# Attention, a rational layer and routed experts: fixed PSUM banks for routing, an early block two steps sooner, and the order of two branches of code

## The chip, the cores and the metric

The kernel runs on one core of one Trainium2 chip. The metric is the device time of one execution in microseconds (us), the median of three runs. The core has five engines with instruction queues of their own: TensorE (PE: matrix products, with the weight loads as PEld), VectorE (DVE), ScalarE (ACT), GpSimd (POOL) and SyncE (SP, which here issues DMAs). Each executes its own queue in order. A wait at the head of a queue holds up all that is queued behind it.

## The reference

Three parts follow one another. An attention with a position bias (4 batches, 8 heads, 576 positions, 64 wide) gives 2304 tokens of 512. A rational layer takes them through 2048 hidden columns, and a routed layer of 8 experts sends each token to the one expert with the largest logit.

```python
def rational(x):                      # 2304 x 512, hidden 2048
    h = x @ w_in
    P = a[0] + a[1] * h + a[2] * h * h + a[3] * h * h * h
    Q = 1.0 + abs(b[0]) * abs(h) + abs(b[1]) * h * h
    return (P / (Q + 1e-6)) @ w_out

def experts(x):                       # 8 experts, 512 -> 1024 -> 512
    logits = x @ w_gate + modality_bias[modality_id]
    e_idx = argmax(logits); gate = softmax(logits)[e_idx]
    for e in range(8):
        out[e_idx == e] = gate * (maximum(x[e_idx == e] @ w1[e], 0) @ w2[e])
```

With these inputs the experts get 0, 8, 0, 0, 2171, 0, 0 and 125 tokens: one gets nearly all, two get a few, five get none. Which is which the kernel learns at run time.

## The kernel before

**Products in two parts.** Where accuracy matters, an operand is split into a rounded part and its remainder, and a product becomes three (high by high, high by remainder, remainder by high).

**The rational layer** (function `moe`) works on six token tiles of 384 tokens (`NTT`, index t from 0) with 16 chunks of hidden columns each (`NF`, index f). One loop runs over steps G = 16 t + f, 0 to 100, and its body writes out the order of work on every engine by hand. In step G, TensorE computes the first product of chunk G (`mm1(G)`, twelve matmuls, line 671) and the second product of an older chunk (`mm2(G - 5)`, twelve matmuls, line 754). Between them ScalarE and VectorE compute the rational function, pair by pair: `first` (ACT, lines 635 to 637), `den` (DVE, 645), `poly` (DVE, 641 and 642), `inv` (ACT, 649 and 650), `quot` (DVE, 654 to 656), `high` (ACT, 660) and `low` (DVE, 664, the remainder). h is read last by `poly`, one step after `mm1`.

**PSUM.** The pool `pst` has eight banks: two of name "tr", two of "av", and two tiles of two banks of name "sc". h of step G is in "av" where G % 3 = 1 (and for G = 3), else in "tr". "sc" holds the sums of `mm2`. A pool hands out the two buffers of a name in turn, and a new tile waits until its buffer's last user is done.

**Routing of a token tile** runs in steps 4 to 9 of the next tile: `evac` (f = 4) copies the sums; `logit` (5), `choice` (6), the first of three `rows` (7: four transposes, line 793, and an ACT copy, 794), `route` (7: the argmax on DVE with an exp on ACT), `place` (8: the place of each token in its expert's table, small products at lines 832 to 841 and DVE work from 843 to 854), the second and third `rows` (8 and 9), `scatter` (9: three indirect DMAs on POOL, line 858) and `put` (9: three POOL scalings and three stores by SP). Each of these products takes its own "av" tile. In the last tile of the loop POOL and ACT also split the weights of the largest expert (`wa_split`, lines 932 and 933), one sixteenth per step.

**The early block.** Rows of the largest expert that are known after five token tiles, 384 of them, are gathered in step 92 (`ids_gather(early)`, line 1021). `block_x` transposes them (line 1033, bank "av"), copies the rounded part on ACT (1036) and the remainder on DVE (1037), for four chunks of 128 columns. `split_h` computes one of eight hidden chunks of them (twelve matmuls, line 1050, then ACT 1059 and DVE 1060). In the loop's steps 97 to 100 these stand between the last `mm2`; the rest, and the routing of the last token tile, follow the loop. `split_y` (line 1071) is the block's second product; before its last part, `block_x` for the next rows needs a gather that waits for the last tile's scatters and stores.

**The experts.** `level(b)`, nested `If`s, works through the largest expert in blocks of 256. Then `large(1)` (line 1378) takes the other experts, largest first. If the first has over 32 tokens (125 here) and the second hasn't (8 here), `block` computes the first and `few`, a generator, the second beside it: `next(beside)` issues its next part. `few` has four parts (products at lines 1343, 1350, 1357 and 1362). Each ends in an indirect store to `out` (lines 1096 and 1365), and a store to `out` waits for the one before it. `chain`, `ahead` and `small` are further `If`s that are not entered with these counts. The code of an `If` stands first, that of its `Else` behind it.

Of the kernel before, what the change touches and what calls it, by code (L numbers as in the profile page):

```python
# [22 lines left out]
P = 128  # L23
# [651 lines left out]
def moe(ctx, tc, k, ins, x2_d, out):  # L675
# [41 lines left out]

    st, c0 = k.st, k.const

    def mm1(G):  # L720
        t, f = divmod(G, NF)
        r = tiles[t]
        if G not in st:
            c = st[G] = K()
            c.h = pb.tile([P, 512], F32, name="av" if G == 3 or G % 3 == 1 else "tr")
            mm1_chunk(nc, k, r, f, c.h)

    g_of_h = Rational(nc, k)
# [36 lines left out]
    def logit(t):  # L765

        r = tiles[t]
        ps = pb.tile([P, 512], F32, name="av")
        for dc in range(4):
            nc.tensor.matmul(ps[32 * dc:32 * dc + 32, 0:NB], k.gate[:, dc], r.x2[:, dc], start=True, stop=True)  # L770
        r.lt = rt.tile([P, NB], F32, name="lt", bufs=1)
        nc.scalar.copy(r.lt, ps[:, 0:NB])

    def choice(t):

        r = tiles[t]
        ps = pb.tile([P, 512], F32, name="av")
        lps = ps[:, 0:3 * NE].rearrange("p (c e) -> p c e", c=3)
        for c in range(3):
            nc.tensor.matmul(lps[:, c], r.lt[:, c * P:(c + 1) * P], k.sum4[:, 0:NE], start=True, stop=True)  # L780
        r.lg = rt.tile([P, 3, NE], F32, name="lg", bufs=1)
        nc.vector.tensor_tensor(r.lg, lps, k.mbias[:, 3 * t:3 * t + 3], ALU.add)

    def rows(t, c):

        r = tiles[t]
        xr = rt.tile([P, 516], F32, name="xr", bufs=3)
        if c == 0:
            r.xr = []
        r.xr.append(xr)  # L790
        ps = pb.tile([P, 512], F32, name="av")
        for dc in range(4):
            nc.tensor.transpose(ps[:, dc * P:(dc + 1) * P], r.x2[:, dc, c * P:(c + 1) * P], k.idf)
        nc.scalar.copy(xr[:, 0:512], ps)
# [31 lines left out]
    def place(t):  # L826

        r = tiles[t]
        ps = pb.tile([P, 512], F32, name="av")
        for c in range(3):  # L830
            o = ps[:, c * NE:(c + 1) * NE]
            nc.tensor.matmul(o, k.lower, r.ohb[:, c], start=True, stop=False)
            for before in range(c):
                nc.tensor.matmul(o, k.ones, r.ohb[:, before], start=False, stop=False)
            nc.tensor.matmul(o, k.ones, k.cum, start=False, stop=True)
        if t >= NTT - 3:

            o = ps[:, 3 * NE:4 * NE]
            for c in range(3):
                nc.tensor.matmul(o, k.ones, r.ohb[:, c], start=c == 0, stop=False)  # L840
            nc.tensor.matmul(o, k.ones, k.cum, start=False, stop=True)
        sl = rt.tile([P, 3, NE], F32, name="sl", bufs=1)
        nc.vector.tensor_tensor(sl, ps[:, 0:3 * NE].rearrange("p (c e) -> p c e", c=3), k.base, ALU.add)
        nc.vector.tensor_tensor(sl, sl, r.oh, ALU.mult)
        sf = rt.tile([P, 3], F32, name="sf", bufs=1)
        nc.vector.tensor_reduce(sf, sl, mybir.AxisListType.X, ALU.add)
        r.si = rt.tile([P, 3], I32, name="si", bufs=2)
        nc.vector.tensor_copy(r.si, sf)
        if t >= NTT - 3:
            k.count = c0.tile([P, NE], F32, name=f"count{t}")  # L850
            nc.vector.tensor_copy(k.count, o)
        if t < NTT - 1:
            for c in range(3):
                nc.vector.tensor_tensor(k.cum, k.cum, r.ohb[:, c], ALU.add)  # L854

    def scatter(t, c):
        si = tiles[t].si
        nc.gpsimd.indirect_dma_start(k.tab[c], bass.IndirectOffsetOnAxis(ap=si[:, c:c + 1].bitcast(U32), axis=0),  # L858
                                     k.ids[:, 3 * t + c:3 * t + c + 1], None)
# [120 lines left out]
    def early_cols():  # L980
        c = K()
        c.xh, c.xl = ([early_tile()[:, :, 0:3 * P] for _ in range(2)] for _ in range(2))
        return c
# [136 lines left out]
    for G in range(NG + 5):  # L1120
# [6 lines left out]
            split_x(t + 1, f - 12)  # L1127
        if G < NG:
            mm1(G)
        if G == NG + 1:  # L1130
            ecol = early_cols()
            block_x(early, ecol, True, (0, 1))
        if G > NG + 1:
            split_h(early, ecol, G - NG - 2, None)

        g, k2 = G - 1, G // 2 - 1
        if G % 2 == 0:
# [16 lines left out]
        for g in (G - 5, G - 4):  # L1154
            if 0 <= g < NG and G == g + (4 if g < 2 else 5):
                mm2(g)
        if G == NG + 1:
            block_x(early, ecol, True, (2, 3))
        if 1 <= t < NTT:
            if f == 4:  # L1160
                evac(t - 1)
            if f == 5:
                logit(t - 1)
            if f == 6:
                choice(t - 1)
            if f == 7:
                route(t - 1)
            if f == 8:
                place(t - 1)
            if f in (7, 8, 9):  # L1170
                rows(t - 1, f - 7)
            if f == 9:
                for c in range(3):
                    scatter(t - 1, c)
                put(t - 1)
        if G == S1 - 3:
            pick()
# [22 lines left out]

    t = NTT - 1
    evac(t)
    split_h(early, ecol, 3, cp)
    logit(t)
    split_h(early, ecol, 4, cp)
    choice(t)
    route(t)
    split_h(early, ecol, 5, cp)
    place(t)
    for c in range(3):  # L1210
        scatter(t, c)
    for c in range(3):
        rows(t, c)
    split_h(early, ecol, 6, cp)
    put(t)
    split_h(early, ecol, 7, cp)
    order()
    for n in range(2):
# [93 lines left out]
    def block(r, c, ws, beside=()):  # L1312

        beside = iter(beside)
        next(beside, None)
        for f in range(8):
            plain_h(r, c, ws, f, cp)
        next(beside, None)
        for f in range(8):
            plain_y(r, ws, f)  # L1320
            if f in (1, 4):
                next(beside, None)
        block_out(r, cp)

# [53 lines left out]
    def large(p):  # L1378
        if p < NE:
            i = (p - 1) % 2  # L1380
            with tc.If(cnt[p - 1] > 32) as many:
                if p == 1:

                    with tc.If(cnt[1] > 32) as two:
                        block(halves[0], hcols[0], wsets[0])
                        chain(1)
                        large(2)
                    with two.Else():
                        block(halves[0], hcols[0], wsets[0], few(halves[1], hcols[1], wsets[1]))
                        chain(1)  # L1390
                        ahead(3)
                        small(3)
                else:
                    columns(p)
                    ahead(p + 1)
                    block(halves[i], hcols[i], wsets[i])
                    chain(p)
                    large(p + 1)
            with many.Else():
                small(p)  # L1400
# [136 lines left out]
```

## Time and profile before

| | us |
|---|---|
| median of 3 runs (lowest to highest) | 1087.4 (1084.71 to 1088.28) |
| the profiled execution: its own time | 1089.3 |
| its span, first to last instruction | 1087.5 |
| TensorE matmul busy | 1021.7 (94%) |
| TensorE weight load busy | 888.3 (82%) |
| VectorE busy | 753.4 (69%) |
| ScalarE busy | 651.1 (60%) |
| GpSimd busy | 281.7 (26%) |
| mean granted clock of TensorE | 0.986 |

Times within the execution are us from the start of the span. The routed layer's loop ends at about 843, the blocks of the largest expert at about 1045. "issue" as a releaser means that the engine waited for nothing that the profile shows; a q behind an engine's name (PEldq, POOLq) marks instructions of its queue that do no work on data, such as branches and semaphore waits. "A <- B" is a wait of A that B ended.

### The profile page before, as it was taken

What the parts mean: (1) busy time and instruction counts of PE and PEld (TensorE: products, weight loads), DVE (VectorE), ACT (ScalarE), POOL (GpSimd) and SP (SyncE); (2) the same over time, 40 slices, a digit from 0 to 9 for tenths busy, and PEclk for the clock granted to TensorE, in tenths of its full rate; (3) what the DMA queues carried; (4) which work ended last, traced back from release to release, by engine and by line L of the source; (5) the groups of instructions that cost most, each with busy time, mean ns of one, the idle gap of its engine ahead of it and who ended that gap; (6) DMA issues with size and microseconds to landing.
All of it is one profiled execution on the core that took longest, in us unless ns stands there. A gap on an engine that the chain in (4) does not pass through costs nothing. (4 is left out here: it accounts for less than half of the span.)

```text
span 1087.5 us, 19123 instructions
## 1 busy us (share of the span) xinstructions
PE 1021.7 (94%) x6804; PEld 888.3 (82%) x6804; DVE 753.4 (69%) x1544; ACT 651.1 (60%) x1283; POOL 281.7 (26%) x449
## 2 busy tenths in 40 slices
PE   6889999999999999999999999999897989999984
PEld 4657777777777779989999999998797879999962
DVE  7978998888888858888978888889884321112200
ACT  6778778878888756767666666666563221122210
POOL 3434343443433300103012021021361142122100
PEclk9999999999999999999999999999998999999998
DMA  5886876775653344005022031041250366211100
GB/s 160 292 263 169 231 239 187 222 204 146 172 157 112 101 166 184 30 1 31 30 20 40 1 30 30 1 30 58 59 98 1 30 219 203 76 48 51 39 24 16
DMA packets 122078, 113.41 MB, mean 104 GB/s; under 512 B 65055, under 2 KB 94495, under 8 KB 121952
## 3 DMA queue, kind: packets, MB, share of 16 engines
q1 hardware_dynamic: 117828, 101.53, 35.0%
q0 software_dynamic: 3728, 10.25, 3.0%
q8 instruction: 63, 1.03, 0.5%
q14 instruction: 63, 0.52, 0.2%
q10 hardware_dynamic: 396, 0.08, 0.0%
HBM read 78.09 MB, written 33.79 MB: 103 GB/s over the span
## 5 line engine op out<-in xcount | busy, mean ns | idle before, releaser
L754 PE MATMUL sc<-gh,w_b 128*128 128x384 f32 x752 | 209.8, 340 | 2.7 <-ACT x L761 2.7
L754 PEld LDWEIGHTS sc<-gh,w_b 128*128 128x128 f32 x752 | 139.5, 190 | 3.3 <-ACT x L761 3.3
L754 PE MATMUL sc<-gl,w_b 128*128 128x384 f32 x376 | 127.9, 340 | 0.1
L393 PEld LDWEIGHTS tr<-idf,e 128*128 128x128 f32 x576 | 80.6, 207 | 49.2 <-issue 25.0
L351 ACT ACTIVATE e<-e,st 128x576 f32<-128x576 f32 x144 | 112.2, 779 | 13.6 <-DVE st L346 11.8
L346 DVE CUSTOM_DVE_ANT_0 e<-sc,bias_s 128x576 f32<-128x576 f32 x144 | 107.6, 748 | 5.1 <-PE sc L330 3.8
L370 ACT COPY aT<-tr 128x512 f32<-128x512 f32 x144 | 84.4, 586 | 44.5 <-PE tr L393 42.7
L1060 DVE SCALAR_TENSOR_TENSOR hl<-tr,hh 128x256 fp32r<-128x256 f32 x56 | 23.8, 425 | 122.8 <-ACT hh L1059 110.6
L671 PE MATMUL tr<-kn,w_a 128*128 128x384 f32 x372 | 107.7, 344 | 0.4 <-DVE t L642 0.4
L393 PE MATMUL tr<-idf,e 128*128 128x128 f32 x576 | 104.6, 304 | 1.7 <-DVE kk L311 0.9
L330 PE MATMUL sc<-kk,qS 128*128 128x288 f32 x512 | 99.1, 315 | 0.7 <-DVE st L346 0.7
L660 ACT CAST gh<-t 128x768 fp32r<-128x768 f32 x47 | 39.3, 835 | 87.8 <-DVE t L656 85.6
L436 PE MATMUL av<-aT,vn 128*64 128x320 f32 (+1 forms) x512 | 82.8, 424 | 0.0
L1050 PE MATMUL tr<-kn,w_a 128*128 128x256 f32 x448 | 81.5, 280 | 1.2 <-DVE hl L1060 1.2
L330 PEld LDWEIGHTS sc<-kk,qS 128*128 128x128 f32 x512 | 72.9, 191 | 2.2 <-DVE st L346 1.0
L858 POOL DMA_INDIRECT tab<-ids,si x18 | 21.6, 1201 | 197.6 <-DVE cum L854 170.3
L754 PEld LDWEIGHTS sc<-gl,w_b 128*128 128x128 f32 x376 | 71.6, 190 | 0.4 <-DVE gl L664 0.4
L671 PEld LDWEIGHTS tr<-kn,w_a 128*128 128x128 f32 x372 | 68.9, 190 | 3.3 <-issue 2.3
L1050 PEld LDWEIGHTS tr<-kn,w_a 128*128 128x128 f32 x448 | 69.7, 188 | 1.7 <-DVE hl L1060 1.4
L1071 PE MATMUL sc<-w_a,hh 128*128 128x512 f32 x224 | 70.9, 393 | 0.0
L366 POOL TENSOR_SCALAR rb<-st 128x128 f32<-128x128 f32 x80 | 23.8, 298 | 170.8 <-DVE st L364 154.2
L654 DVE SCALAR_TENSOR_TENSOR t<-t,coef,r 128x768 f32<-128x768 f32 x47 | 48.2, 1025 | 24.6 <-ACT r L650 24.6
(303 smaller groups left out, 2539.2 us busy)
## 6 DMA issues: line engine op xcount, KB each, us to landing
bias_d<-bo SPq DMA_DIRECT2D x36, 295.5 KB
kn<-in_k_dram SPq DMA_DIRECT2D x64, 128.0 KB
cst<-in_moe_w_out_dram SPq DMA_DIRECT2D x16, 512.0 KB
wo_d<-cvw SPq DMA_DIRECT2D x16, 512.0 KB
cst<-in_moe_w_in_dram SPq DMA_DIRECT2D x16, 512.0 KB
w_b<-wo_d SPq DMA_DIRECT2D x16, 512.0 KB
w_b<-in_moe_w_dram SPq DMA_DIRECT2D x16, 512.0 KB
x_d<-xr SPq DMA_DIRECT2D x18, 256.5 KB
```

The lines of the kernel that those rows point to most:

```text
L330: nc.tensor.matmul(ps[:, hf, 0:HF], st, mv[:, hf * HF:(hf + 1) * HF], start=n == 0, stop=n == last)
L346: nc.vector.tensor_tensor_reduce(out=ev, in0=ps[:, :, 0:HF], in1=bv, scale=-1.0, scalar=3.0e38, op0=ALU.add, op1=ALU.min, accum_out=st[:, ...
L351: nc.scalar.activation(e, e, AF.Exp, bias=st[:, 0:1], scale=-1.0, accum_out=st[:, 1:2])
L370: nc.scalar.copy(dst, src)
L393: nc.tensor.transpose(ps[:, c * P:(c + 1) * P], both[:, e0 + c % 2:e0 + 2 * P:2], k.idf)
L436: nc.tensor.matmul(r.av[64 * hd:64 * hd + 64, 0:w], st, mv, start=c == 0, stop=c == 4)
L654: nc.vector.scalar_tensor_tensor(q.t, q.t, co[:, 0:1], q.r, ALU.add, ALU.mult)
L660: self.nc.scalar.copy(gh, q.t)
L671: nc.tensor.matmul(h[:, 0:k.NB], k.wi[f][:, wv, dc * P:(dc + 1) * P], xv[dc], start=n == 0, stop=n == 11)
L754: nc.tensor.matmul(r.acc[dc][:, 0:NB], wo[f][:, wv, ws], gv, start=f == 0 and n == 0, stop=f == NF - 1 and n == 2)
L1050: nc.tensor.matmul(ps[:, 0:n], w[:, wv, cs], xv[dc // 2][:, dc % 2], start=j == 0, stop=j == 11)
L1071: nc.tensor.matmul(r.acc[a], r.h[f][hv][:, cs], wa[8 + f][:, wv], start=f == 0 and n == 0, stop=f == 7 and n == 2)
```

## The change

- Two "av" banks are allocated once for the loop. h goes to bank G % 3 of them (in effect one of the two, but for G = 3), all routing products to the other. From step 95 on the fixed tiles are given up, and "av" tiles are taken in turn again.
- The second and third `rows` stand in steps 9 and 10 in place of 8 and 9, `put` in step 10 in place of 9.
- `early_cols` and `block_x` of the early block move from step 97 (chunks 0 and 1 ahead of `mm2`, 2 and 3 behind it) to steps 95 (chunk 0), 96 (1 and 2) and 97 (3), each behind `mm2`. `split_h` 0 and 1 move from steps 98 and 99, ahead of `mm2`, to 97 and 98, behind it; number 2 moves from step 100 to behind `evac`. Behind the loop the routing steps of the last tile stand one `split_h` sooner in the order.
- In `block`, the later parts of `few` are issued after chunk 3 of the first product, after the first product, and after chunk 1 of the second (before: after the first product, and after chunks 1 and 4 of the second).
- In `large(1)`, the condition on the second expert is turned round, so that the code with `few` stands first and the code for a large second expert in the `Else`.

```diff
+    fixed = [pb.tile([P, 512], F32, name="av") for _ in range(2)]
+
+    def routing_bank():
+        return fixed[0] if fixed else pb.tile([P, 512], F32, name="av")
...
-            c.h = pb.tile([P, 512], F32, name="av" if G == 3 or G % 3 == 1 else "tr")
+            c.h = fixed[G % 3] if G == 3 or G % 3 == 1 else pb.tile([P, 512], F32, name="tr")
...
-        ps = pb.tile([P, 512], F32, name="av")
+        ps = routing_bank()
...
-        if G == NG + 1:
-            ecol = early_cols()
-            block_x(early, ecol, True, (0, 1))
-        if G > NG + 1:
-            split_h(early, ecol, G - NG - 2, None)
...
+        if G == NG - 1:
+            fixed.clear()
+            ecol = early_cols()
+            block_x(early, ecol, True, (0,))
+        if G == NG:
+            block_x(early, ecol, True, (1, 2))
         if G == NG + 1:
-            block_x(early, ecol, True, (2, 3))
+            block_x(early, ecol, True, (3,))
+        if G in (NG + 1, NG + 2):
+            split_h(early, ecol, G - NG - 1, None)
...
-            if f in (7, 8, 9):
-                rows(t - 1, f - 7)
+            if f in (7, 9, 10):
+                rows(t - 1, {7: 0, 9: 1, 10: 2}[f])
             if f == 9:
                 for c in range(3):
                     scatter(t - 1, c)
+            if f == 10:
                 put(t - 1)
...
     evac(t)
+    split_h(early, ecol, 2, cp)
+    logit(t)
     split_h(early, ecol, 3, cp)
-    logit(t)
-    split_h(early, ecol, 4, cp)
     choice(t)
     route(t)
-    split_h(early, ecol, 5, cp)
+    split_h(early, ecol, 4, cp)
     place(t)
     for c in range(3):
         scatter(t, c)
     for c in range(3):
         rows(t, c)
+    split_h(early, ecol, 5, cp)
+    put(t)
     split_h(early, ecol, 6, cp)
-    put(t)
     split_h(early, ecol, 7, cp)
...
             plain_h(r, c, ws, f, cp)
+            if f == 3:
+                next(beside, None)
         next(beside, None)
         for f in range(8):
             plain_y(r, ws, f)
-            if f in (1, 4):
+            if f == 1:
                 next(beside, None)
...
-                    with tc.If(cnt[1] > 32) as two:
-                        block(halves[0], hcols[0], wsets[0])
-                        chain(1)
-                        large(2)
-                    with two.Else():
+                    with tc.If(cnt[1] < 33) as one:
                         block(halves[0], hcols[0], wsets[0], few(halves[1], hcols[1], wsets[1]))
                         chain(1)
                         ahead(3)
                         small(3)
+                    with one.Else():
+                        block(halves[0], hcols[0], wsets[0])
+                        chain(1)
+                        large(2)
```

## Rows read from the trace of the kernel before

**Rows 1.** The page's busy times: us, share of the span, instructions.
```profile
PE 1021.7 (94%) x6804; PEld 888.3 (82%) x6804; DVE 753.4 (69%) x1544; ACT 651.1 (60%) x1283; POOL 281.7 (26%) x449
```
**Rows 2.** Table by stretches: length, each engine's busy time, PEclk, DMA share, GB/s.
```profile
825.00:835.00 10.00, 6.76 (x22) 6.18 (x21) 4.16 (x6) 2.60 (x5) 1.29 (x1) 0.68 0.00 0
875.00:885.00 10.00, 7.89 (x43) 7.00 (x44) 2.19 (x4) 3.67 (x7) 6.17 (x13) 0.83 0.51 110
1050.00:1054.00 4.00, 4.00 (x20) 1.82 (x17) 0.67 (x2) 0.75 (x2) 0.98 (x1) 0.57 0.20 71
```
**Rows 3.** TensorE's waits from 470 to 880: total us, times, longest.
```profile
PE av L793 <- DVE cum L854: 4.2, 1, 4.2
PE av L1033 <- DMA xg<-x_d,tixg: 2.9, 2, 1.8
...
PE av L671 <- DVE cum L854: 1.4, 1, 1.4
PE av L793 <- DVE sl L843: 1.2, 1, 1.2
PE av L793 <- DVE t L642: 1.1, 1, 1.1
```
**Rows 4.** VectorE's waits from 470 to 735, token tiles 1 to 4.
```profile
DVE t L654 <- ACT r L650: 13.9, 18, 0.8
DVE q L645 <- ACT q L636: 9.7, 19, 1.1
DVE lg L782 <- PE av L780: 5.3, 4, 1.4
```
**Rows 5.** VectorE in order of time: start, duration, line [idle before <- releaser].
```profile
789.65 1.02 DVE L645 SCALAR_TENSOR_TENSOR q<-q,coef,e 128x768 f32<-128x768 f32 x1 [1.81 <-ACT q L636]
...
822.75 1.02 DVE L1037 TENSOR_TENSOR w_b<-av,w_b 128x384 fp32r<-128x384 f32 x2 [1.64 <-ACT w_b L1036]
...
828.52 1.01 DVE L1037 TENSOR_TENSOR w_b<-av,w_b 128x384 fp32r<-128x384 f32 x2
```
**Rows 6.** TensorE in order of time: one hidden chunk of the early block.
```profile
839.20 2.25 PE L1050 MATMUL tr<-w_b,w_a 128*128 128x384 f32 x12
```
**Rows 7.** Branches and drains by line: ns min/median/max, first and last start.
```profile
L1384 PEldq COMPARE_BRANCH  x1: 3515/3515/3515, 1045.6 to 1045.6; - x1
...
L1370 PEldq COMPARE_BRANCH  x2: 3513/4240/4968, 1073.3 to 1077.0; - x2
...
L1370 POOLq COMPARE_BRANCH  x2: 38/42/45, 1083.1 to 1084.3; - x2
...
L1533 POOLq DRAIN  x3: 40/111/900, 1085.7 to 1087.2; - x3
...
L1533 PEldq DRAIN  x2: 8/36/63, 1082.0 to 1087.0; - x2
```
**Rows 8.** The tail in order of time: TensorE, ScalarE, GpSimd.
```profile
1049.65 3.67 PE L1343 MATMUL av<-w_b,x 128*32 128x512 f32 x16 [4.56 <-issue]
...
1064.34 1.92 PE L1357 MATMUL av<-w_b,hh 128*32 128x512 f32 x16
...
1072.82 0.69 ACT L1095 ACTIVATE y<-sc,xr 128x512 f32<-128x512 f32 x1 [2.05 <-PE sc L1090]
...
1076.22 1.00 POOL L1096 DMA_INDIRECT out_dram<-y,tlh  x1 [3.72 <-ACTq L1370]
```
**Rows 9.** Token tile 5 in order of time: first row transposes and their copy.
```profile
770.70 0.60 PE L793 MATMUL av<-idf,x 128*128 128x128 f32 x4
...
775.45 0.57 ACT L794 COPY xr<-av 128x512 f32<-128x512 f32 x1
```
**Rows 10.** The early gather's last part, such parts' landing time, the gh cast.
```profile
809.98 0.95 POOL L1021 DMA_INDIRECT qt<-x_d,tie  x1 [0.30 <-issue]
...
qs<-x_d,tie POOLq DMA_INDIRECT x4, 3.8
...
816.14 0.83 ACT L660 CAST gh<-t 128x768 fp32r<-128x768 f32 x1 [2.64 <-DVE t L656]
```

More of the change, by code (lines that the diff above doesn't have):

```diff
@@ L776, in choice @@
         r = tiles[t]
-        ps = pb.tile([P, 512], F32, name="av")
+        ps = routing_bank()
         lps = ps[:, 0:3 * NE].rearrange("p (c e) -> p c e", c=3)
@@ L790, in rows @@
         r.xr.append(xr)
-        ps = pb.tile([P, 512], F32, name="av")
+        ps = routing_bank()
         for dc in range(4):
@@ L828, in place @@
         r = tiles[t]
-        ps = pb.tile([P, 512], F32, name="av")
+        ps = routing_bank()
         for c in range(3):
```

## The prediction

> **What bounds the kernel now.** I read the page's busy times first. TensorE is busy 94% of the span [rows 1], but a busy matmul row isn't work at full clock, so I went on to the granted clock by stretches [rows 2] and to what TensorE waits for [rows 3]. The reader should see two things there. The waits are few, and nearly all lie in the places that this diff edits. And behind some of them the clock is halved: 0.68, 0.83 and 0.57 of 2.4 GHz in three stretches, where the level was 1.2 GHz for part of the time after TensorE had waited. Third, I read who waits for whom on VectorE [rows 4]: in the rational layer VectorE and ScalarE form a closed loop, and TensorE and that loop hold each other up at the routing of every token tile. Last, the end of the layer, the branches and the tail [rows 5 to 8]. So the bound is TensorE's order of work, except in the last token tile, where ScalarE's and GpSimd's splitting of the expert weights slows the loop and the loop sets the pace.
>
> The sum is made against the profiled execution: 1087.5 us of span, 1089.3 us as its own time, so 1.8 us lie around the span. The median of the runs shown is 1087.4 (1084.71 to 1088.28). I take the gain off the median.
>
> **Term A, the fixed banks in token tiles 1 to 4.** Now the routing products share two rotating banks with a third of the h tiles, and TensorE waits after `place` until VectorE has read its bank: 1.4, 1.2 and 1.1 us in three of the tiles [rows 3]; 3.7 us is the most that can come back. With h on its own bank, and the second group of row transposes one step later, that wait has a whole step to pass in. But TensorE gains only what the loop gains. VectorE waits for the `choice` product 5.3 us in four tiles, and at that place would otherwise wait for ScalarE's reciprocal, 0.77 us a time (13.9 over 18) [rows 4]; of the 2.2 us difference I count 1.9, since tile 1 has no earlier saving. VectorE's waits for ScalarE before the denominator are 9.7 us in 19 [rows 4], the longest behind row copies that wait for late transposes; I take 1.5 of them, an estimate. A = 3.4, between 0 and 3.7.
>
> **Term B, the same in tile 5.** TensorE's 4.2 us wait before the second row transposes [rows 3] goes, but the loop is late there, so TensorE meets it again at the next pair. What counts is VectorE's 1.81 us wait at 789.65 [rows 5], which stems from ScalarE holding a row copy for TensorE. I take 0.75, between 0 and 1.8: the copy, no longer waiting, still costs its own time.
>
> A single bank also adds waits: each product now waits for its predecessor's reader. In tile 5 the first row transposes stand at 770.70 and their copy ends at 776.02, 5.3 us later [rows 9], more than a step (24 products; twelve take 2.25 [rows 6], so about 4.4). `place` waits for that, and the loop hides it as above. Elsewhere I cost it at nothing; the step between the products is the cover, and the rival below prices its loss.
>
> **Term C, the early block's columns.** They move from step 97 to steps 95 to 97, the first two products of the expert layer from 98 to 100 to 97 and 98. Now TensorE runs transposes, waits, and starts the first product only to wait again for the last column chunk, whose two VectorE copies run from 828.52 to 829.53, right behind the last pair's remainder [rows 5]. After the change one copy stands there, not two, but it stands in the same place behind the same remainder: `block_x` for chunk 3 needs the bank of chunk 1, and its ScalarE copy is queued behind the last gh cast. I gain half of 1.01 and two products that no longer follow, about 0.6 at half clock: C = 1.1. VectorE's 1.64 us wait at 822.75 for two chunk copies ahead of the last quotient [rows 5] stays, since chunks 1 and 2 stand in that place now. Bounds: -3.4 and +3, how much longer or shorter the clock is low (0.68 over the ten us [rows 2], so 3.2 us lost there now).
>
> New is that the transposes need the gather two steps sooner. Its last part is issued at 809.98 and such a part lands 3.8 us after issue, at about 813.8; ScalarE reaches the place of the first chunk copy at about 817, behind the cast at 816.14 [rows 10]. That cast hides it; TensorE may stand idle there, but it would wait for the loop in any case. Past that cover every us would be lost by all three engines. `put` goes one step later, with three scalings on GpSimd and three stores on SP, ahead of the id loads; the gather comes two steps behind, behind the weight splits, and these cover it.
>
> **Term D, the routing of the last tile.** With two products done before `evac`, only one stands ahead of `logit`, as now, but the whole routing chain, its scatters, `put` and the gather of the next rows start one product (2.25 us [rows 6]) sooner against TensorE's own work, which is the same in sum. TensorE now waits 2.9 us for that gather [rows 3], 0.7 is left; and of the clock lost behind it, 1.7 us of the ten at 0.83 [rows 2], I take 1.4 as work. D = 2.2 + 1.4 = 3.6, between 1.5 and 4.3.
>
> **Term E, the tail.** TensorE's branch to the few-token code takes 3.515 us [rows 7], most of the 4.56 us before the first product there [rows 8]; code placed first is run on into. I count 3.4. The first part then runs at half clock, 3.67 us against 1.92 for the same sixteen products later [rows 8]: 1.75 more. `few` also ends three steps of the second product earlier, so the last scatter needn't wait for the scatter before it: it starts at 1076.22, though its y is ready at 1073.51 [rows 8], 2.7 us. Against it stands a new jump over the other code at the end. TensorE's two there take 3.5 and 5.0 [rows 7]; I take 4.2. TensorE reaches the final drain at 1082.0, GpSimd at 1085.7 [rows 7], so TensorE's end would be 1082.0 - 5.15 + 4.2 = 1081.0, and GpSimd's 1085.7 - 5.15 - 2.7 + its own jump (0 to 5.0; I take 1.4, as from its last branch at 1084.3 to the drain) = 1079.3. The later one counts: E = 4.7, between 0.2 and 5.4.
>
> The Trainium skill's page "Runtime: NRT & Kernel Launch", section "Instruction fetch mechanics", says that a taken branch whose target isn't among the pages already loaded must wait for a fetch. The 3.515 us agree. By that rule alone the jump is moved, not removed: see the second rival.
>
> **Sum**: 3.4 + 0.75 + 1.1 + 3.6 + 4.7 = 13.5, so 1073.9 us. With all upper ends, 3.7 + 1.8 + 3 + 4.3 + 5.4 = 18.2: 1069.
>
> **The rivals.** First, the loop keeps its pace: VectorE and ScalarE don't gain from an earlier TensorE, the waits turn up again at mm2's remainders, and A, B and C are nothing. For it: the loop's waits in the layer are mostly its own (13.9 and 9.7 against 5.3 [rows 4]). Against it: the 5.3 is for TensorE alone. Time 1087.4 - 3.6 - 4.7 = 1079.1.
>
> Second, the far jump is only moved: at the end GpSimd pays 5.0 and the scatter gains nothing, E = 0.2, time 1078.4. For it: the jumps there are as dear as the one removed [rows 7]. Against it: TensorE has 3.7 us of room there, and the half clock behind the old jump is gone in any case. The same time comes if the few-token code isn't run on into. Both rivals together, with D at its lower end, give 1087.4 - 1.5 - 0.2 = 1085.7, no change.
>
> Third, slower: one bank for all routing. A product waits for its predecessor's reader in each of five tiles. It decides when the reader ends more than about 1.9 us beyond a step, 6.3 us after the product, in every tile: then five waits outweigh C, D and E (9.4). With 2.6 us a tile, 1087.4 - 9.4 + 13 = 1091. For it: 5.3 us in tile 5 [rows 9]. Against it: the other tiles have no weight splits and are earlier.
>
> **How the numbers follow.** Forecast 0.61; first rival 0.17; second 0.12; both together 0.06; slower 0.04. About 0.3% (3.3 us) is what a measurement of this kernel can tell from no change. Faster: 0.61 + 0.17 + 0.12 = 0.90, less 0.02 for a sum in the forecast's lower bounds: 0.88. Same: 0.06 + 0.02 = 0.08. Slower 0.04. The range goes from 1069 (all upper ends) over both single rivals to 1083, which leaves out the last two cases.
>
> **What would show it.** A: no TensorE wait after `place`, shorter VectorE waits on `choice`. B and C: the last remainder ends some 4 us sooner, and the last chunk copy right behind it. D: TensorE's wait for the gathered rows under 1 us and full clock behind it. E: the few-token branch under 0.2 us, the first product within about 1.2 us of the last expert matmul; three far branches at TensorE's end. I am wrong if the gather lands behind the gh cast, if row copies hold TensorE in tiles 1 to 4, or if the end chain grows by as much as the tail shrinks.

## The result, and the profile after

The changed kernel takes 1070.6 us (median of 4 runs, 1069.92 to 1072.28), the kernel before 1087.6 on the same chip (4 runs): ratio 0.9849, 95% interval 0.9831 to 0.9868, so 17.0 us faster. The profiled execution has 1070.2 us of its own and a span of 1068.4, against 1087.5 before, 19.1 apart. Of these, 2.4 us lie ahead of the routed layer, in attention code that wasn't changed: the layer's first remainder on VectorE ends at 409.5 us in the trace of before and at 405.7 to 408.1 in the other traces, which all have the same attention code. All comparisons by stage below count from that end.

The page after, busy times (us, share of the span, instructions):

```profile
PE 1017.6 (95%) x6804; PEld 885.4 (83%) x6804; DVE 754.4 (71%) x1544; ACT 651.0 (61%) x1283; POOL 280.8 (26%) x449
```

The work is that of [rows 1]; what shrank is waiting and half clock (stretches in which TensorE was granted 1.2 of its 2.4 GHz): the mean granted clock rose from 0.986 to 0.991. TensorE's waits from 470 to 880 us (total us, times, longest):

```profile
PE tr L1055 <- ACT w_b L1041: 3.7, 1, 3.7
...
PE av L1038 <- DVE w_b L1042: 2.5, 2, 1.7
...
PE av L798 <- ACT xr L799: 1.8, 2, 1.1
PE av L1038 <- DVE t L642: 1.1, 1, 1.1
PE av L1038 <- DMA qt<-x_d,tie: 1.1, 1, 1.1
PE av L1038 <- DMA xg<-x_d,tixg: 1.1, 1, 1.1
...
PE tr L1055 <- DVE w_b L1042: 0.4, 1, 0.4
```

Against [rows 3], every wait of TensorE for VectorE behind `place` is gone (from 470 to 735 us TensorE waits for nothing), and the wait for the gathered rows (`tixg`) fell from 2.9 to 1.1. At the top stands a new longest wait: the first expert product (L1055) waits 3.7 us for ScalarE's copy of the last column chunk (L1041). And `block_x` now waits 1.1 us for the early gather (`tie`). Start, duration, line [idle before <- releaser]:

```profile
806.43 0.33 PE L1038 MATMUL av<-idf,qt 128*128 128x128 f32 x1 [1.07 <-DMA qt<-x_d,tie]
...
808.90 0.83 ACT L660 CAST gh<-t 128x768 fp32r<-128x768 f32 x1 [2.60 <-DVE t L656]
...
809.63 0.47 ACT L1041 CAST w_b<-av 128x384 fp32r<-128x384 f32 x1
```

This wait is hidden, as the prediction said: ScalarE copies the chunk at 809.63, behind the gh cast, 3.2 us after the gather had released TensorE, and TensorE then waits for VectorE again (the 1.1 us of `DVE t L642`). VectorE's waits from 470 to 735, to be read beside [rows 4]:

```profile
DVE t L654 <- ACT r L650: 14.7, 19, 0.8
DVE q L645 <- ACT q L636: 6.2, 19, 0.7
DVE lg L787 <- PE av L785: 4.4, 4, 1.1
```

The table by stretches (length, each engine's busy time, PEclk, DMA share, GB/s), beside [rows 2]:

```profile
806.00:830.00 24.00, 15.90 (x74) 14.31 (x75) 14.53 (x17) 9.05 (x17) 4.85 (x4) 0.86 0.00 1
...
850.00:880.00 30.00, 28.09 (x166) 24.36 (x165) 6.69 (x23) 6.22 (x15) 11.38 (x24) 1.00 0.64 115
```

The clock is full now in the stretch ahead of level 0 (0.83 for ten of its us before), but still low for part of the stretch with the chunks. Branches and drains (ns min/median/max, first and last start), which answer [rows 7]:

```profile
L1397 PEldq COMPARE_BRANCH  x1: 68/68/68, 1034.2 to 1034.2; - x1
...
L1383 PEldq COMPARE_BRANCH  x2: 3729/4323/4917, 1057.2 to 1061.2; - x2
...
L1383 POOLq COMPARE_BRANCH  x2: 38/42/45, 1063.0 to 1064.0; - x2
...
L1546 POOLq DRAIN  x3: 40/107/911, 1066.7 to 1068.2; - x3
...
L1546 PEldq DRAIN  x2: 8/38/68, 1066.2 to 1067.9; - x2
```

The branch to the few-token code fell from 3515 to 68 ns. At the end of TensorE stand two far branches, as before, not three; its drain is now 0.5 us ahead of GpSimd's (3.7 before). GpSimd, which ends last, takes 2.7 us from its last branch to its drain (1064.0 to 1066.7), 1.4 before (1084.3 to 1085.7 [rows 7]). The tail in order of time, beside [rows 8]:

```profile
1035.15 2.37 PE L1356 MATMUL av<-w_b,x 128*32 128x512 f32 x16 [1.50 <-ACTq L1276]
...
1056.78 0.69 ACT L1100 ACTIVATE y<-sc,xr 128x512 f32<-128x512 f32 x1 [4.62 <-PE sc L1095]
...
1058.55 1.00 POOL L1101 DMA_INDIRECT out_dram<-y,tlh  x1 [4.68 <-issue]
```

The first part of `few` takes 2.37 us in place of 3.67. The last scatter starts 1.8 us after ScalarE begins its y, before 3.4.

By stage, each kernel's difference to the kernel before in us at seven points, all counted from the end of the layer's first remainder, from one trace each. "tile 5" is the end of the eighth-last remainder, "level 0" the start of the first product of the next block, "end" the end of the span, the others are starts. The experiments are told below:

| | tile 5 | first split_y | level 0 | last split_y | first few product | last scatter | end |
|---|---|---|---|---|---|---|---|
| before (us) | 344.8 | 448.8 | 471.0 | 635.2 | 640.2 | 666.8 | 678.0 |
| after | -4.35 | -5.3 | -8.2 | -9.1 | -12.1 | -15.3 | -16.7 |
| after, again | -4.25 | -5.25 | -8.0 | -8.85 | -11.9 | -15.2 | -16.5 |
| placement alone | 0.0 | +1.4 | +1.0 | +0.9 | -2.1 | -4.1 | -5.55 |
| both tail edits | 0.0 | +0.7 | +0.4 | -0.5 | -3.6 | -6.8 | -7.0 |
| banks and row steps | -4.25 | -6.2 | -5.1 | -4.9 | -4.5 | -4.6 | -4.65 |
| early order alone | +0.05 | -0.4 | -3.3 | -4.1 | -3.8 | -4.0 | -6.3 |
| banks alone | +2.4 | +0.8 | +0.4 | -0.3 | -0.1 | -0.7 | -0.9 |
| row steps alone | -4.1 | -4.9 | -5.1 | -5.2 | -4.9 | -5.3 | -6.7 |
| after, without early order | -4.1 | -7.4 | -7.95 | -8.8 | -11.8 | -15.1 | -16.4 |
| chunks two and two | -4.1 | -10.9 | -13.3 | -14.15 | -17.2 | -20.5 | -21.8 |
| two and two, late splits | -4.3 | -13.7 | -16.1 | -17.0 | -20.0 | -23.3 | -23.5 |
| two and two, no banks | -4.2 | -10.8 | -13.5 | -14.3 | -17.4 | -20.6 | -21.7 |

The two traces of after lie within 0.25 us of each other at every point. Two cautions all the same. The stretch from the last scatter to the end is 11.2 us in before and 8.9 in the kernel with the early order alone, whose tail is the same: about 2 us there belong to the execution, and the landing of that scatter's store makes them (5.7 us after its start in before, 3.2 there). And half clock comes and goes between executions of one kernel: over all 138 timed runs, within a kernel, a mean clock lower by 0.001 goes with 0.7 us more (slope of a straight line; correlation -0.71). So small differences of a single trace are read only where a wait explains them.

### The profile page after: what moved, and what is told of

It is laid out like the page before. It is cut to its first block, busy times and chain, and to the rows that moved or that the text cites. A ratio compares the mean times of both kernels' runs of the same rounds, so it can differ in the third digit from the quotient of the medians.

```text
span 1068.4 us, 19126 instructions
## 1 busy us (share of the span) xinstructions
PE 1017.6 (95%) x6804; PEld 885.4 (83%) x6804; DVE 754.4 (71%) x1544; ACT 651.0 (61%) x1283; POOL 280.8 (26%) x449
## 5 line engine op out<-in xcount | busy, mean ns | idle before, releaser
L351 ACT ACTIVATE e<-e,st 128x576 f32<-128x576 f32 x144 | 112.2, 779 | 13.3 <-DVE st L346 11.4
L1055 PE MATMUL tr<-kn,w_a 128*128 128x256 f32 x448 | 81.6, 280 | 0.9 <-ACT w_b L1100 0.7
L1055 PEld LDWEIGHTS tr<-kn,w_a 128*128 128x128 f32 x448 | 69.7, 188 | 1.7 <-ACT w_b L1100 1.1
```

The source lines that it names most:

```text
L351: nc.scalar.activation(e, e, AF.Exp, bias=st[:, 0:1], scale=-1.0, accum_out=st[:, 1:2])
L1055: nc.tensor.matmul(ps[:, 0:n], w[:, wv, cs], xv[dc // 2][:, dc % 2], start=j == 0, stop=j == 11)
```

## Experiments: the parts one at a time

**Placement.** The few-token code first, nothing else.

```diff
-                    with tc.If(cnt[1] > 32) as two:
-                        block(halves[0], hcols[0], wsets[0])
-                        chain(1)
-                        large(2)
-                    with two.Else():
+                    with tc.If(cnt[1] < 33) as one:
                         block(halves[0], hcols[0], wsets[0], few(halves[1], hcols[1], wsets[1]))
...
+                    with one.Else():
+                        block(halves[0], hcols[0], wsets[0])
+                        chain(1)
+                        large(2)
```

> The kernel before with one edit: the few-token code is placed first and the two-large-experts code after it; few keeps its old positions. Theory (the branch goes, and no jump of its own comes at TensorE's end): the branch row of 3.5 us on TensorE falls to under 0.1 us, the half clock behind it goes (1.3 us, as in the kernel after), two far branches stand before TensorE's final drain as before, and the last scatter still starts behind its predecessor: 4 to 5 us faster than before, 0.3 to 0.5%. Rival (the jump is only moved, as my prediction charged 4.2 us for it): a third far branch of 3.5 to 5 us at the end of TensorE, drain near that of before: 0 to 1.3 us faster.

Measured: ratio 0.9951 (0.9936 to 0.9967), 5.3 us faster, a little over the theory's 4 to 5. The far branches of TensorE at its end in this kernel:

```profile
L1370 PEldq COMPARE_BRANCH  x2: 3866/4532/5197, 1066.9 to 1071.0; - x2
```

Two, as before. On TensorE, then, the jump was removed and not moved. The Trainium skill's page "Runtime: NRT & Kernel Launch", section "Instruction fetch mechanics", lets a taken branch out of the loaded pages wait for a fetch; the 3.9 and 5.2 us here agree with that. That a third such branch must come at TensorE's end was my own step, and no row bears it out. Why the trace has no third I can't show; in the order of the code, the end of the few-token branch leads straight to the end of the branch around it, so that one jump could do for both. That is argued only. On GpSimd, though, part of the jump did come back:

```profile
L1370 POOLq COMPARE_BRANCH  x2: 38/42/45, 1074.1 to 1075.1; - x2
...
L1533 POOLq DRAIN  x3: 40/107/917, 1077.5 to 1079.0; - x3
```

From its last branch to its drain GpSimd takes 2.4 us here, 1.4 in before. In the five traces with the old order of the code this stretch is 1.3 to 1.6 us, in the eight with the new order 2.4 to 2.9, some 1.2 more. That this is its own jump over the code that now stands behind is likely, but not tested.

**Both edits of the tail**: as above, and the second part of `few` behind chunk 3 of the first product, the fourth behind chunk 1 of the second.

> The kernel before with both edits of the tail: few-token code first, and few's second and third parts at their new positions. Theory (the tail's edits make the whole of term E as the trace of after shows it): 7 to 8 us faster than before (0.65 to 0.75%), that is some 3 us more than with the placement alone, since the last scatter no longer waits for the one before it and lands 3.3 instead of 5.7 us after its issue. Rival (TensorE's end binds, the scatter's start is worth nothing): the same time as the placement alone, 4 to 5 us faster than before.

Measured: ratio 0.9928 (0.991 to 0.9945), 7.8 us faster, as expected; but the two intervals overlap slightly. Up to the last scatter the tail gains 6.3 us from the last expert product on (-0.5 to -6.8), with the placement alone 5.0, so `few`'s positions bring 1.3 in the traces and 2.5 by the ratios. The last scatter's landing, which the theory put at 3.3 us in place of 5.7, took 4.5.

**Banks and row steps**, with the early block and the tail as before.

> The kernel before with the fixed banks, the second and third row transposes at steps 9 and 10 and the put at step 10; early block and tail as before. Theory (terms A and B as the trace of after shows them): the waits of TensorE behind place in token tiles 1 to 4 are gone, VectorE waits 1 us less for choice, nothing more is gained in tile 5: 4 to 5 us faster than before (about 0.4%). Rival (the loop of VectorE and ScalarE keeps its pace): TensorE's waits turn up again at the mm2 remainders of the same tiles, under 1 us faster.

Measured: ratio 0.9924 (0.9904 to 0.9945), 8.2 us faster, nearly twice what I expected. Tile 5 starts 4.25 us sooner, as in after, so that part of the theory holds and the rival falls. The rest of the trace gains nothing lasting, but that execution was one of the longest of its kernel (1082.2 against a median of 1078.9), with a mean clock of 0.983; over its runs the mean is 0.986, and over those of before beside it 0.983.

**Banks alone, and row steps alone.** The first has the fixed banks with `rows` at 7, 8, 9; the second is this:

```diff
-            if f in (7, 8, 9):
-                rows(t - 1, f - 7)
+            if f in (7, 9, 10):
+                rows(t - 1, {7: 0, 9: 1, 10: 2}[f])
...
+            if f == 10:
                 put(t - 1)
```

> The kernel before with the fixed banks alone; the row transposes stay at steps 7, 8 and 9, put at 9. Theory (term A needs both: the later step gives the single bank's reader its time): the second group of transposes stands right behind place on the same bank, so TensorE waits there in every one of the four tiles, 1 to 1.5 us each, and the layer's four tiles take as long as before or up to 2 us longer. Rival (taking h off the routing banks is what removes the waits): the start of token tile 5 comes 4.3 us sooner, as with banks and steps together.

> The kernel before with the second and third row transposes at steps 9 and 10 and put at 10 alone, banks rotating as before. Theory (a step between place and the next product on its bank is what removes the wait): the waits behind place go in tiles 1 to 4 and the start of token tile 5 comes 3 to 4.3 us sooner. Rival (the h tile in the rotation is what hands the bank back late): the waits stay at 1.1 to 1.4 us in three tiles, only one step later; start of tile 5 under 1 us sooner.

Measured: banks alone 1.0002 (0.998 to 1.0024), row steps alone 0.9938 (0.9917 to 0.9959). TensorE's waits from 470 to 880, first two lines of the banks alone, then two of the row steps alone:

```profile
PE av L798 <- DVE count L856: 5.9, 2, 4.1
PE av L798 <- DVE sl L848: 3.6, 3, 1.2
```

```profile
PE av L793 <- DVE t L642: 0.8, 1, 0.8
PE av L793 <- ACT xr L794: 0.7, 1, 0.7
```

With one bank and the old steps, the row transposes wait for VectorE's reading of `place` in all five tiles. With the old rotation and the new steps that wait is gone. Tile 5 starts 4.1 us sooner by the steps alone and 4.25 with the banks: term A is the row steps' work, and the fixed banks bring 0.15 us in these two traces, too little to count. For the row steps the theory held; for the banks too, but that their 2.4 us at tile 5 are a little over the 2 that it allowed, and have 1.7 us of half clock in them.

**Early order alone**: the columns at steps 95 to 97, the first products at 97 and 98 and the order behind the loop; banks, row steps and tail as before.

> The kernel before with the early block's column chunks at steps 95 to 97, its first products at 97 and 98 and the order of work behind the loop as in the kernel after; banks, row steps and tail as before. Theory (terms C and D don't need the banks): second product of step 93 starts 1 us sooner, the wait for the gathered rows falls from 2.9 to about 1 us and the half clock before the first weight split of level 0 goes: 3.5 to 4.5 us faster than before. Rival (what I booked as C and D comes from the earlier tiles' banks, which free the loop for the early columns): 0 to 1.5 us faster, or slower, with TensorE waiting over 3 us at the early chunk for a loop that is late.

Measured: ratio 0.9983 (0.9971 to 0.9995), 1.8 us faster, about half of the theory: the interval, 0.5 to 3.2 us, leaves out the theory's 3.5 to 4.5 and takes in part of the rival's 0 to 1.5. In the trace the theory holds for D up to level 0 (2.9 us, and 0.8 behind it) but not for C (0.4 us, and that with 1.7 us less lost to half clock than in before):

```profile
PE tr L1050 <- ACT w_b L1036: 3.7, 1, 3.7
...
PE av L1033 <- DMA xg<-x_d,tixg: 1.1, 1, 1.1
```

The wait for the gathered rows is down to 1.1, as in after. The wait for the last chunk is up from 2.6 to 3.7. The profiled run was the fastest of 12, the median 5 us above it; what the slower executions lack, one trace can't show.

**After, without the early order.**

> The kernel after with the early block's columns, its first products and the order of work behind the loop as in the kernel before: banks, row steps and both edits of the tail stay. Theory (term C is nothing or a small loss, term D is 3.7 us of which 2.9 lie between the first split of the second product and level 0): second product of step 93 starts 0 to 1 us sooner than in the kernel after, level 0 some 2 to 3 us later, the whole 2.5 to 3.5 us slower than the kernel after, that is 13.5 to 14.5 us faster than before (ratio 0.987). Rival (C is worth the 1.0 us that I read from the two traces, on top of D): the second product of step 93 starts 1 us later than in the kernel after, 4.5 to 5 us slower than it, 12 us faster than before (ratio 0.989).

Measured: ratio 0.9881 (0.9859 to 0.9903), 13.0 us faster, between the theory (0.987) and the rival (0.989). The trace speaks against the rival: the first split_y stands 2.1 us sooner without the early order (-7.4 against -5.3), so the columns lose there, and more than the theory said. TensorE's waits of this kernel:

```profile
PE av L1038 <- DMA xg<-x_d,tixg: 3.3, 2, 2.1
...
PE tr L1055 <- ACT w_b L1041: 1.4, 1, 1.4
```

The wait for the last chunk is 1.4 in place of 3.7, the wait for the gathered rows 3.3 in place of 1.1. What the early order gains behind the first split_y it loses ahead of it: 0.3 us are left at the end in the traces, 3 to 4 in the ratios, whose intervals overlap. The profiled run of this kernel was its fastest of six (1071.5, median 1073.7), so its trace may show the early order's worth too low.

## Experiments: what holds the last tile

In after, the last chunk's copy stands behind the last gh cast in ScalarE's order. Start, duration, line [idle before <- releaser]:

```profile
820.16 0.83 ACT L660 CAST gh<-t 128x768 fp32r<-128x768 f32 x1 [4.26 <-DVE t L656]
820.90 0.47 ACT L1041 CAST w_b<-av 128x384 fp32r<-128x384 f32 x1
821.03 0.96 DVE L664 TENSOR_TENSOR gl<-t,gh 128x768 fp32r<-128x768 f32 x1 [0.90 <-ACT gh L660]
821.42 0.69 PE L1055 MATMUL tr<-w_b,w_a 128*128 128x384 f32 x1 [3.66 <-ACT w_b L1041]
...
823.31 0.52 PE L759 MATMUL sc<-gh,w_b 128*128 128x384 f32 x1
```

**Chunks two and two**:

```diff
         if G == NG - 1:
             fixed.clear()
             ecol = early_cols()
-            block_x(early, ecol, True, (0,))
+            block_x(early, ecol, True, (0, 1))
         if G == NG:
-            block_x(early, ecol, True, (1, 2))
-        if G == NG + 1:
-            block_x(early, ecol, True, (3,))
+            block_x(early, ecol, True, (2, 3))
```

> The kernel after with the early block's column chunks 0 and 1 at step 95 and chunks 2 and 3 at step 96, none at 97. Theory (in the kernel after the last chunk's ScalarE copy at 820.9 us behind the last gh cast is what holds the first product, 3.7 us of TensorE's wait): that wait goes, TensorE waits for the last remainder of VectorE instead (its end at 822.0 against the second product's start at 823.3), so that the second product of step 93 starts 1 to 1.5 us sooner and the whole is 1 to 3 us faster than the kernel after, depending on whether the half clock there stays; ratio to before 0.982 to 0.984. Rival (the copies only change places on ScalarE and VectorE ahead of the last quotient, so the loop ends later by what TensorE gains): second product of step 93 at the same time, ratio 0.985.

Measured: 1064.6 us, ratio 0.9803 (0.978 to 0.9827), better than the theory, whose better end the interval still takes in. The second product of step 93 starts 3.6 us sooner (counted from the layer's first remainder), not 1 to 1.5. The same place in this kernel:

```profile
814.93 0.84 ACT L1041 CAST w_b<-av 128x384 fp32r<-128x384 f32 x2
...
816.62 2.25 PE L1055 MATMUL tr<-w_b,w_a 128*128 128x384 f32 x12
...
818.71 0.33 PE L759 MATMUL sc<-gh,w_b 128*128 128x384 f32 x1
...
820.79 2.25 PE L1055 MATMUL tr<-w_b,w_a 128*128 128x384 f32 x12
...
821.43 0.96 DVE L664 TENSOR_TENSOR gl<-t,gh 128x768 fp32r<-128x768 f32 x1 [0.90 <-ACT gh L660]
...
822.88 0.33 PE L759 MATMUL sc<-gh,w_b 128*128 128x384 f32 x1
```

Here my expectation had a wrong step. I took the second product behind the first expert product to need VectorE's last remainder. It doesn't: it starts at 818.71, before that remainder begins. Only the next one (822.88) reads it, and by then two expert products and a second product have filled TensorE's time. Nothing had to wait there at all; the 3.7 us in after were the chunk's copy alone. Term C, too, took the copy's place behind the last gh cast as given and priced only its length. TensorE's waits at the chunks and the first product sum up to 8.8 us in after (3.7, 2.5, 1.1, 1.1 and 0.4) and to 4.5 here (3.2, 1.0 and 0.3). Half clock stays, 3.4 us lost in either: at 820.7 to 827.6 us in after, at 807.3 to 814.2 here, where it begins within the wait that is left. The first split_y comes 5.6 us sooner than in after, and all of it behind the third-last remainder: up to there the two traces are level (394.0 and 394.1 us from the layer's first remainder), although after has a stretch of half clock at 752 us that this execution lacks.

**Late splits.** What is left is a wait of 3.2 us of the second chunk for VectorE (`PE av L1038 <- DVE t L642`). On the version above:

```diff
-        i = G - S1 - 2
-        if 0 <= i < 16:
+        for i in {98: (11, 12), 99: (13, 14), 100: (15,)}.get(G, (G - S1 - 2,) if 0 <= G - S1 - 2 < 11 else ()):
             wa_tile(i)
             wa_split(i, spec[i], nc.gpsimd)
```

> The kernel with column chunks two and two (0 and 1 at step 95, 2 and 3 at 96), and besides the splits of the expert weights 11 to 15, which only the second expert product needs, moved from steps 93 to 97 to steps 98 to 100. Theory (the loop of the last tile is slow because of the splits: 0.6 us each on ScalarE, and VectorE's operations beside one on GpSimd take 1.5 to 2.1 us instead of 1.0; that is why term B came to nothing): the pairs from step 93 on take 1 to 2 us less each, VectorE's last remainder ends 2 to 4 us sooner, TensorE's wait of 3.2 us at the second chunk shrinks by 1 to 3 us, the whole is 1 to 4 us faster than with the chunks two and two alone, ratio to before 0.977 to 0.9795. Rival (the loop is slow by its own chain, the splits lie in its gaps): the last remainder ends within 0.7 us of where it did, ratio 0.980; and at steps 98 to 100 the splits would hold up the copies of evac: up to 2 us slower.

Measured: 1063.2 us, ratio 0.9782 (0.9753 to 0.981). The interval doesn't part theory and rival, the traces do. First the pair of that place with the splits beside it (chunks two and two), then without:

```profile
803.49 1.49 DVE L654 SCALAR_TENSOR_TENSOR t<-t,coef,r 128x768 f32<-128x768 f32 x1 [0.77 <-ACT r L650]
804.11 1.99 POOL L938 TENSOR_TENSOR w_a<-x,w_a 128x512 fp32r<-128x512 f32 x1
805.01 1.90 DVE L655 SCALAR_TENSOR_TENSOR r<-q,one,r 128x768 f32<-128x768 f32 x1
...
816.37 2.11 DVE L654 SCALAR_TENSOR_TENSOR t<-t,coef,r 128x768 f32<-128x768 f32 x1
816.37 1.29 POOL L938 TENSOR_TENSOR w_a<-x,w_a 128x512 fp32r<-128x512 f32 x1 [4.00 <-ACT w_a L937]
```

```profile
804.05 1.02 DVE L654 SCALAR_TENSOR_TENSOR t<-t,coef,r 128x768 f32<-128x768 f32 x1 [0.77 <-ACT r L650]
805.10 1.02 DVE L655 SCALAR_TENSOR_TENSOR r<-q,one,r 128x768 f32<-128x768 f32 x1
...
808.28 0.44 PE L1038 MATMUL av<-idf,qs 128*128 128x128 f32 x2 [1.04 <-DVE t L642]
...
814.45 1.01 DVE L654 SCALAR_TENSOR_TENSOR t<-t,coef,r 128x768 f32<-128x768 f32 x1
...
818.41 0.96 DVE L664 TENSOR_TENSOR gl<-t,gh 128x768 fp32r<-128x768 f32 x1 [0.90 <-ACT gh L660]
```

VectorE's quotient takes 1.02 us where no split runs on GpSimd and 1.49 to 2.11 beside one, and the slow ones end some 0.82 us behind the GpSimd operation that they met (ends at 806.10 and 806.91, at 817.66 and 818.48). The last remainder ends 4.2 us sooner (counted from the layer's first remainder, which ends 1.2 us later in this trace), TensorE's wait falls from 3.2 to 1.0, and the first split_y comes 2.8 us sooner, 1.7 of them from less half clock behind the shorter wait. `evac` isn't held up. So the splits do slow the loop of the last tile.

**No banks, and after again**, on the chip of the late splits. The first is the version with chunks two and two, with all `routing_bank()` tiles and `fixed` taken out again.

> The kernel with column chunks two and two, but without the fixed banks: the routing products and the h tiles rotate over the two banks as in the kernel before; the later row steps, the early products and the tail stay. Theory (the fixed banks are worth 0 to 0.3 us, the later row steps carry term A): start of token tile 5 within 0.4 us of the kernel with the banks, whole time within 1 us of it, ratio to before 0.980 to 0.982. Rival (the banks are needed once the early columns come into the loop, since h and the chunks share the rotation): TensorE waits again at h or at the chunks, 2 us or more slower, ratio 0.982 or more.

> The kernel after, unchanged, on the chip of the two runs beside it, so that the versions can be compared with it there. Theory (chips differ less than the versions): ratio to before 0.983 to 0.987, that is 4 to 6 us slower than with the chunks two and two. Rival (the gain of the chunks two and two was the chip's): the three ratios within 0.002 of each other.

Measured: without banks 1064.3 us, ratio 0.979 (0.976 to 0.9821); after again 1070.6, ratio 0.9847 (0.982 to 0.9875). The fixed banks aren't needed for any of the gain. On this one chip after stands 6.3 us behind the two-and-two order without banks, and 7.4 us behind the version with late splits as well, which is the lowest of this study, though the 1.1 us between these two aren't clear of the spread.

## Why the prediction was right, and where its steps were not

Forecast 1073.9, measured 1070.6, inside the range of 1069 to 1083. The sum, 13.5, missed 3.2 of the 16.7 us in the layer and the tail: 2.9 in term E, 0.95 in A, and -0.7 in the other three. Two lines of the kernel before bear on it that weren't shown so far, a wait of TensorE from the view of [rows 3] and, from the chain that ended last, the store ahead of the last scatter until it landed:

```profile
PE av L671 <- DVE sl L843: 0.7, 1, 0.7
```

```profile
1071.61 2.57 DMA out_dram<-y,tlh
```

- **A**, forecast 3.4 with 3.7 as its upper end, measured 4.35 at tile 5. The bound left out the fourth wait behind `place`, the 0.7 us, in tile 1; with it the waits sum to 4.4, and nearly all of that came back. VectorE's side was mis-sized both ways: its wait for `choice` fell by 0.9 (5.3 to 4.4) and not by the 1.9 that I counted, its waits ahead of the denominator by 3.5 (9.7 to 6.2) and not by 1.5, and those for the reciprocal grew by 0.8. The cause was named only in half: I spoke of the bank and the step together, and the step does it.
- **B**, forecast 0.75, and **C**, forecast 1.1, together 1.85; measured 0.97, 0.5 between tile 5 and the third-last remainder, 0.5 from there to the first split_y. The parts are not what I said, so that the sum comes within 1 us is luck. Without the early order the first split_y comes 3.3 us sooner from tile 5 on: 0.5 up to the third-last remainder, 2.85 behind it, of which 1.7 are less half clock; the other 1.1 I had booked nowhere, and what makes them isn't shown. The columns cost 2.1 there (-5.3 with them, -7.4 without, 3.4 us lost to half clock in either) instead of gaining 1.1. The step that failed is the sentence that one copy stands behind the last remainder where two stood, and so half is saved: the copy's place behind the gh cast decides, not its length, and with all chunks ahead of it (two and two) TensorE's waits there fell from 8.8 to 4.5 us. The gather was hidden by its cast, as forecast.
- **D**, forecast 3.6, measured 2.9 up to level 0 and 0.9 behind it, 3.8. The wait for the gathered rows fell by 1.8, to 1.1 and not to 0.7. The 2.9 are well shown: from the first split_y to level 0 the seven traces with the old order take 21.7 to 23.4 us, the six with the early order 19.3 to 19.8. The 0.9 are not. From level 0 to the last split_y the four traces with half clock just ahead of level 0 take 164.2 to 164.4 us, all others 163.3 to 163.6; but of the seven with the old order three (both tail edits, banks alone, after without early order) had no half clock there either.
- **E**, forecast 4.7, measured 7.6 in the trace. Its parts up to the last scatter: 3.1 for the branch (3.4), 1.55 for half clock and the parts of `few` (1.75), 1.6 for the scatter (2.7). Of these 2.7 us between the end of its y and the scatter, 1.1 are there in after too (1057.47 to 1058.55), and in before the store ahead had landed 0.7 us behind that end, at 1074.18: the scatter's wait for it was a small part of them. The mis-sized term is the charge of 4.2 for a third far branch at TensorE's end, which would have made TensorE the last by 1.7 us. It doesn't exist; without it the prediction's own sum gives 1085.7 - 1079.3 = 6.4 for E. The 1.4 that it took for GpSimd's own jump came about (1.3). The remaining 1.4 lies between the last scatter and the end, where executions differ by 2 anyway: the last store lands 2.4 sooner after its start than in before (3.3 against 5.7), GpSimd's way to its drain takes 1.3 longer.
- **Rivals.** The loop doesn't keep its pace (banks and row steps gain). The jump isn't moved on TensorE (placement gains 5.3), only some 1.2 us of it on GpSimd, and of these at most 0.5 count in after, where TensorE's drain stands 0.5 ahead. One bank doesn't make it slower with the steps; with the old steps it costs 2.4 us at tile 5, so that rival named a real mechanism, whose cover is the later step.

Open: why TensorE has no third far branch, what the 1.2 us on GpSimd are, and how much of the early order's gain stays over many executions (0.3 us in the traces, 3 to 4 in the ratios).

## What to carry to other kernels

When a product waits for a bank, first move it a step away from the bank's reader; here that alone gave the whole of term A, and a private bank for it nothing. When work is moved forward into a loop, look at which instruction it stands behind on the copying engine: a half-microsecond copy behind a cast that waits for the loop cost TensorE 4 us of waits. Before charging a new wait or jump, ask of the trace which later instruction truly reads the late result.

## What was not expected of the hardware

- VectorE operations on 128x768 take 1.02 us alone and up to 2.11 beside a GpSimd operation on 128x512 (1.3 to 2.0 us); moved apart, they were back at 1.02. In the traces of before, after, chunks two and two and late splits, 127 of VectorE's scalar_tensor_tensor on 128x768 took over 1.15 us, and every one ends 0.81 to 0.83 us behind the end of a GpSimd tensor operation that it overlaps: it looks as if it stood still until that one was done.
- The same program's mean granted clock ran from 0.978 to 0.987 over the runs of before, and its time from 1081.8 to 1091.6 us; after and the three versions with chunks two and two stay at 0.990 to 0.995 and spread less (after 1068.5 to 1072.3).
- Turning round a condition took a branch of TensorE from 3515 to 68 ns without a further long one on TensorE; GpSimd's way from its last branch to its drain grew from 1.3 to 1.6 us to 2.4 to 2.9.
